# K rows of a long-convolution kernel: regrouped through DRAM in five reads a quarter, position zero joined to the skip weight, new issue order

## The chip, the cores and the metric

The program runs on one core of one Trainium2 chip. Times are device microseconds (us) of one execution. A kernel is run several times; the text gives the median and says how many runs there were. Most runs agree within 1 to 1.5%; a run more than 1.5% above the fastest of its kernel is marked slow and left out of ratios. Each kernel was also profiled once. A "span" is that execution from its first to its last instruction; it is about 2 us shorter than the time.

The engines: PE is TensorE (matmul), DVE is VectorE, ACT is ScalarE, POOL is GpSimd, SP is SyncE, which in this kernel does nothing but start DMA transfers. "SPq" in the profile is SyncE's sequencer at work on starting a transfer.

## The reference

Two independent halves are concatenated: a linear attention over x (2048 x 448, 16 heads), and a long convolution of u (2048 x 448) with a kernel K that a state-space model gives. Only the second half is touched:

```python
# _B_ref, cut
dt = jnp.exp(log_dt)[:, None];  A = A_re + 1j * A_im
l = jnp.arange(L)                                          # L = 2048
P = jnp.exp((dt * A)[:, :, None] * l[None, None, :])
K = jnp.einsum("dn,dnl,dn->dl", Cc, P, dt * Bc).real       # 448 channels x 2048 positions
... # FFT of K and u, both padded to 2L, product, inverse FFT
y = y + u * Dskip[None, None, :]
```

In bf16, `arange(2048)` holds only 641 different values, so the kernel computes K at 641 positions.

## The kernel before

The 448 channels are done in four quarters of 112. For each quarter, VectorE builds tables of powers, TensorE multiplies a "high" table (16 rows) with a "low" table (49 columns) to get K at position HI + LO, and ScalarE evicts that to the tile TS. In TS a partition is one high position of one of four channel groups. The spectrum matmuls want the K positions themselves on the partitions: the tile KT. `scatter_k` moves TS to KT. Position zero is the one that fits no block of 128 rows; it has a sixth block, KT[:, 5], with one row in use.

```python
N_LO = 49
K_ROWS = [(0, 0, 8, 0, 16), (1, 0, 8, 16, 32), (2, 8, 16, 16, 32), (3, 0, 16, 33, 41), (4, 0, 16, 41, 49)]
N_KT = 6
...
def dma(eng, o, i):
    e = {"S": nc.sync, "AD": nc.scalar, "G": nc.gpsimd}[eng]
    prog.add(eng, lambda: e.dma_start(out=o, in_=i))
...
def scatter_k(qt):                                  # one "set": 24 transfers, all on SyncE
    ts_, kt_ = TS[qt % 2], KT[qt % 2]
    for kt, h0, h1, l0, l1 in K_ROWS:
        for g in range(4):
            dma("S", kt_[:, kt, 28 * g:28 * g + 28], ts_[32 * g + h0:32 * g + h1, l0:l1, :])
    for g in range(4):                              # position zero: 4 transfers of 56 bytes
        dma("S", kt_[0:1, 5, 28 * g:28 * g + 28], ts_[32 * g:32 * g + 1, 32, :])
...
def query_side(sc):                                 # the attention half, cut
    ...
    dma("S", SCd[sc], SCT)                          # a small tile out to DRAM ...
    for h in range(4):                              # ... and back, spread over partitions
        dma("S", SB[28 * h:28 * h + 28], bass.AP(...SCd...))
    for s in range(2):
        mul(EQ[:, s], EQ[:, s], SB[:, 4 * s:4 * s + 4, :])     # VectorE waits for it
...
TERMS = ([(0, 0), (1, 1), (2, 2), (3, 3), (4, 5)], [(5, 3), (6, 4)])   # spectrum matmuls per K block
def load_f(m, at):                                  # the F tables of the spectrum, also SyncE
    t = sb(at, [128, 2, 7, 128])
    dma("S", t, F_d[m])
```

The program records its 1,198 operations and then issues them in a hand-tuned order (`ORDER`), with PSUM banks from a second list (`SLOTS`). SyncE works its transfers off in that order: one that waits, or that takes long to start, holds up all that come after it. In the profile of this kernel, SyncE was busy with the 24 starts of a set from 161.16 for 16.27 us, and started the query side's small transfer, next in its order, at 177.53, 0.10 us after the last of them.

The softmax here doesn't subtract the row's maximum and nothing guards it: scores larger than these inputs give would overflow.

Of the kernel before, what the change touches and what calls it, by code (L numbers as in the profile page):

```python
# [16 lines left out]
D_MODEL = 448  # L17
# [3 lines left out]
N_LO = 49  # L21
# [5 lines left out]
LO = [s * p for p in LO_ABS[:-1] for s in (1, -1)] + [16, 0, -16]  # L27
LO += [512 + p for p in LO[24:32]]
LO += [2 * LO[i] for i in (35, 37, 38, 40)]
LO += [512 + p for p in LO[41:45]]  # L30
assert len(LO) == N_LO
HI = [16 + 32 * a for a in range(N_HI)]
K_ROWS = [(0, 0, 8, 0, 16), (1, 0, 8, 16, 32), (2, 8, 16, 16, 32), (3, 0, 16, 33, 41), (4, 0, 16, 41, 49)]
N_KT = 6
# [6 lines left out]
def _row_positions():  # L41
    pos = np.full((N_KT, 128), -1)
    for kt, h0, h1, l0, l1 in K_ROWS:
        pos[kt] = [HI[h] + LO[lo] for h in range(h0, h1) for lo in range(l0, l1)]
    pos[5, 0] = HI[0] + LO[32]
    return pos

def _dft_tables():
# [10 lines left out]
    assert len(where) == 641 and set(where) == set(e.tolist())  # L59
    F = np.zeros((2, N_KT, 128, 4, 512))  # L60
    for blk in range(2):
        for l in range(1024):
            kt, r = where[int(e[1024 * blk + l])]
            even = np.exp(-1j * w * l) / 1024.0
            odd = np.exp(1j * (np.pi - w) * l) / 1024.0
            F[blk, kt, r] += np.stack([even.real, odd.real, even.imag, odd.imag])
    used = [(0, 0), (0, 1), (0, 2), (0, 3), (0, 5), (1, 3), (1, 4)]
# [4 lines left out]
    FT = FT.reshape(7, 128, 2, 8, 128).transpose(3, 1, 2, 0, 4)  # L72
# [31 lines left out]
def kernel(  # L104
# [22 lines left out]
    SUd = dram.tile([4, 128, 8, D_MODEL], BF16, name="SUd")  # L127
    SCd = dram.tile([4, 128, 128], BF16, name="SCd")
# [212 lines left out]
    for part, terms in enumerate(([("CreBre", DG), ("CimBim", DGN)], [("CreBim", DG), ("CimBre", DG)])):  # L341
        bs = prog.take("P", *((6, 7), (2, 3))[part])
        to_states(bs, [(prods[n], d) for n, d in terms])
        acopy(halves(CR[:, part, :]), two(bs))
    for n, k in enumerate(LOWP):
# [73 lines left out]
    dma("G", DSK, bass.AP(tensor=B_Dskip.tensor, offset=B_Dskip.offset, ap=[[0, 128], [1, D_MODEL]]))  # L419
# [3 lines left out]
    for kt in KT:  # L423
        mset(kt[:, 5, :], 0.0)
# [7 lines left out]
    def amps(qt):  # L432
        return sb((oW, 174336, 174336, oW)[qt], [128, 33, QC])
# [25 lines left out]
    def dampings(qt):  # L459
        A = amps(qt)  # L460
        for grp in range(2):
            p0, far_ = args(AT, qt, grp)
            for _, n, f, r0, step in GROUP[grp]:
                for sgn in (1, -1):
                    r = 2 * r0 + (sgn < 0) if r0 < 15 else (30, 32)[sgn < 0]
# [9 lines left out]
    def damp(qt, x0, w):  # L475
        A = amps(qt)
        smul(W[:, 1, 0:31:2, x0:x0 + w], A[:, 0:31:2, x0:x0 + w], -1.0)
        for part in (1, 0):
            for r, n, d, tr in ((0, 15, QC, 0), (30, 1, 2 * QC, 15)):
# [9 lines left out]
                else:  # L489
                    mul(view(o, [d, 2], [1, w]), view(a, [step, 2], [1, w]), view(b, [0, 2], [1, w]))  # L490
# [4 lines left out]
    def far(qt, x0, w):  # L495
# [10 lines left out]
        def four(part):  # L506
            return view(W[:, part, 35, x0:x0 + 1], [3 * QC, 2], [2 * QC, 2], [1, w])
# [7 lines left out]
        step(24, 33, 8)  # L515
# [3 lines left out]
        mul(view(W[:, 1, 41, x0:x0 + 1], [2 * QC, 2], [QC, 2], [1, w]), four(0), four(1))  # L519
        smul(rows_(1, 41, 4), rows_(1, 41, 4), 2.0)  # L520
        sub(rows_(0, 41, 4), sq[0], sq[1])
        step(41, 45, 4)
# [38 lines left out]
    def scatter_k(qt):  # L561
        ts_, kt_ = TS[qt % 2], KT[qt % 2]
        for kt, h0, h1, l0, l1 in K_ROWS:
            for g in range(4):
                dma("S", kt_[:, kt, 28 * g:28 * g + 28], ts_[32 * g + h0:32 * g + h1, l0:l1, :])
        for g in range(4):
            dma("S", kt_[0:1, 5, 28 * g:28 * g + 28], ts_[32 * g:32 * g + 1, 32, :])
# [100 lines left out]
    TERMS = ([(0, 0), (1, 1), (2, 2), (3, 3), (4, 5)], [(5, 3), (6, 4)])  # L668

    def load_f(m, at):  # L670
        t = sb(at, [128, 2, 7, 128])
# [153 lines left out]
    "0 2 15 4 3 5 22 21 12 14 9 6 11 10 28 17 27 7 8 13 1 19 29 16 20 30 18 31 32 33 23 43 24 36 44 25 51 26 159 "  # L825
    "52 91 157 89 37 92 90 56 53 34 99 55 97 127 66 100 129 35 54 75 57 85 98 58 81 76 88 61 82 79 80 87 77 45 78 "
    "84 83 86 40 209 38 227 64 46 65 59 236 70 218 41 68 60 62 69 130 103 63 161 104 160 93 212 101 95 102 162 42 "
    "165 96 221 49 94 128 208 354 39 50 226 105 210 47 106 107 48 357 72 112 108 211 109 113 73 158 74 71 213 114 "
    "214 110 215 217 136 111 230 117 115 135 219 116 220 180 119 164 181 67 222 122 223 118 224 183 120 182 235 "
    "184 121 123 124 185 186 239 187 216 125 225 245 229 126 188 228 244 237 231 254 238 232 133 233 253 134 240 "  # L830
    "234 248 139 241 247 242 246 257 249 243 140 137 250 256 251 255 189 252 138 258 131 262 163 132 141 259 271 "
    "260 265 191 264 261 177 274 273 147 178 276 267 298 263 148 268 277 190 266 166 179 272 172 142 269 170 193 "
    "174 171 270 192 143 275 144 168 278 173 279 145 280 176 146 152 169 167 175 283 205 207 153 282 281 206 285 "
    "194 284 286 154 195 287 200 197 290 432 433 288 293 435 434 301 436 289 300 292 303 299 291 302 294 316 201 "
    "155 307 295 296 199 326 156 304 203 305 202 297 368 306 310 343 318 438 309 437 319 312 308 198 317 321 311 "
    "320 325 322 196 323 473 313 204 314 149 474 370 329 372 369 475 315 150 476 327 151 479 328 477 470 478 330 "
    "324 471 531 481 331 332 472 334 371 480 333 337 335 336 525 338 346 344 345 429 347 348 527 418 339 431 340 "
    "341 349 342 424 350 427 374 351 423 425 422 353 426 356 352 420 355 484 483 421 373 358 485 482 359 419 534 "
    "376 428 375 378 362 379 377 486 380 363 488 487 489 430 490 366 381 528 383 367 360 491 364 361 492 382 365 "
    "493 677 526 384 511 385 494 439 392 495 530 390 532 397 391 529 394 440 520 499 496 498 395 497 521 441 533 "  # L840
    "398 443 407 536 399 535 389 518 387 516 403 442 513 386 396 519 408 515 388 445 406 393 402 514 444 415 404 "
    "512 537 500 540 412 517 539 416 501 400 414 401 411 413 538 405 541 542 410 409 543 504 570 417 630 631 459 "
    "451 460 450 454 453 452 447 458 449 544 446 448 456 462 545 457 522 461 455 505 463 546 465 469 464 467 468 "
    "466 547 506 524 633 632 634 523 548 508 507 569 502 509 671 678 549 679 566 550 668 672 567 674 669 673 616 "
    "553 551 554 676 552 627 670 675 718 625 568 681 682 572 680 683 715 626 624 620 684 635 622 686 685 629 555 "
    "712 503 556 628 709 510 619 687 898 559 688 689 618 899 690 636 571 623 557 617 560 558 574 563 621 573 576 "
    "561 577 575 578 564 579 691 562 761 581 719 565 580 582 720 583 716 750 692 710 637 693 602 711 604 717 608 "
    "600 714 639 603 713 695 694 697 696 598 638 754 722 724 641 721 601 751 723 610 762 593 613 725 763 727 605 "
    "726 728 590 729 757 730 585 760 596 731 758 640 756 732 614 759 592 752 611 584 755 733 595 699 734 753 612 "
    "597 698 606 594 607 589 599 643 737 736 588 738 735 609 642 586 615 587 702 767 591 659 660 661 664 665 658 "  # L850
    "666 662 663 657 656 654 646 667 655 648 706 645 653 703 647 652 644 649 650 651 700 707 764 740 704 701 739 "
    "814 705 925 765 708 741 815 745 817 766 743 853 816 860 768 769 924 742 747 744 818 770 748 842 854 846 746 "
    "956 749 855 771 856 820 861 772 773 864 775 774 825 881 776 866 777 865 862 778 863 821 871 779 823 843 888 "
    "872 873 780 819 847 781 845 844 828 829 848 791 849 790 831 824 830 926 928 850 927 827 832 793 867 851 795 "
    "834 852 833 822 882 835 826 883 889 884 836 892 891 837 857 893 894 839 806 874 859 807 858 890 802 895 838 "
    "788 897 896 868 785 870 841 869 875 840 878 876 786 880 929 800 879 877 808 885 787 886 930 803 887 931 798 "
    "792 932 809 933 804 943 810 783 811 782 942 801 799 784 805 796 789 944 794 1038 812 797 967 1070 1072 963 "
    "1073 1071 946 949 961 945 962 948 969 947 934 968 935 959 1057 953 965 957 960 970 950 1042 1004 964 813 "
    "1043 966 903 918 915 902 911 958 917 914 936 923 919 916 905 901 913 922 907 908 906 920 909 904 954 910 921 "
    "912 900 1041 971 951 955 939 937 1039 952 938 973 940 1040 941 972 974 976 975 1082 977 978 979 1078 981 980 "  # L860
    "982 1083 1005 1079 1084 1080 1085 1007 1076 1081 983 1074 984 985 987 986 1006 1002 1008 989 1009 1075 1077 "
    "1000 991 1010 1001 990 1011 992 998 1012 1013 999 1015 1014 988 1016 994 1017 1018 996 997 1019 993 1003 "
# [43 lines left out]
```

## Time and profile before

The median was 373.94 us (three runs, 373.57 to 377.03); the profiled run: span 373.4 us.

| engine | busy us | share of the span |
|---|---|---|
| DVE | 268.4 | 72% |
| PE | 252.3 | 68% |
| ACT | 209.7 | 56% |

No engine is full. DVE has the most work, and still stands idle for 373.4 - 268.4 = 105 us. The question is what it stands idle for. First the page of the kernel before: span, busy times, and the chain that ended last, by engine and by line.

```profile
span 373.4 us, 8746 instructions
PE 252.3 (68%) x3781; PEld 188.8 (51%) x3781; DVE 268.4 (72%) x324; ACT 209.7 (56%) x346; POOL 15.9 (4%) x32
PE 9%; SPq 8%; DVE 7%; issue 2%; DMA 1%; ACT 1%; DVEq 0%; ACTq 0%
PE psum L198 9%; SPq L213 8%; DVE sbuf L159 7%; DMA sbuf<-sbuf 1%; ACT sbuf L190 1%; DVEq L159 0%; ACTq L190 0%
```

Line 213 is the helper `dma`. The shares sum to 28% because the chain is followed back only to 267.4 us, so it covers the last two sets alone. That SyncE's sequencer has 8% of the last chain, with 1% for the transfers themselves, says that starting them is what counts. The view of line 213 gives one such start (count, then ns minimum/median/maximum, first and last start):

```profile
L213 SPq DMA_DIRECT2D sbuf<-sbuf x96: 567/602/987, 161.2 to 342.8; - x96
```

There are 96 of them (4 sets of 24), and each keeps SyncE for about 0.6 us. The packets of one such transfer took only 0.25 to 0.42 us in the trace, in the 68 of the 80 transfers of 128 packets whose packets stand apart there. The timeline of the kernel before shows the four places where that hurts (start us, length us, engine, what, count; in brackets the engine's idle time before it and what ended that):

```profile
161.16 16.27 SPq L213 DMA_DIRECT2D sbuf<-sbuf  x24
177.53 0.47 SPq L213 DMA_DIRECT2D SCd<-sbuf  x1
189.95 2.36 DVE L159 TENSOR_TENSOR sbuf<-sbuf 112x2048 bf16<-112x2048 bf16 x2 [11.93 <-DMA sbuf<-SCd]
...
241.54 2.45 SPq L213 DMA_DIRECT2D sbuf<-const  x4
246.06 5.84 PE L198 MATMUL psum<-sbuf 128*128 128x224 bf16 x44 [8.06 <-DMA sbuf<-const]
...
281.44 9.21 PE L198 MATMUL psum<-sbuf 128*128 128x112 bf16 x136 [0.84 <-DVE sbuf L159]
284.72 16.42 SPq L213 DMA_DIRECT2D sbuf<-sbuf  x24
302.56 9.82 PE L198 MATMUL psum<-sbuf 128*128 128x112 bf16 x259 [11.90 <-DMA sbuf<-sbuf]
...
326.66 16.70 SPq L213 DMA_DIRECT2D sbuf<-sbuf  x24
344.82 7.39 PE L198 MATMUL psum<-sbuf 128*128 128x112 bf16 x115 [12.11 <-DMA sbuf<-sbuf]
```

Set by set. The first set (161.2 to 177.4) has the query side's small transfer to DRAM behind it in SyncE's order; VectorE waits 11.93 us for what comes back. The second set (it ends at 240.2) has the loads of the F tables behind it (`sbuf<-const` at 241.54); PE waits 8.06 us. The third and the fourth are waited for directly: 11.90 and 12.11 us of PE. The view of waits adds them up for the whole span (us in total, times, longest):

```profile
PE psum L198 <- DMA sbuf<-sbuf: 24.0, 2, 12.1
PE psum L198 <- DMA sbuf<-const: 8.1, 1, 8.1
DVE sbuf L159 <- DMA sbuf<-SCd: 12.6, 2, 11.9
```

The sum of these three, 24.0 + 8.1 + 12.6 = 44.7 us, adds waits of two engines, so it is a count, and not by itself a proof of what they cost. It is called the *set waits* below: the time that PE or DVE stood waiting for K rows, or for something queued behind them.

### The profile page before, as it was taken

The numbers are of one execution on the slowest core, as the hardware profiler recorded it, in microseconds if no ns is written. First come the engines' busy times: TensorE is split into PE (matmuls) and PEld (weight loads), VectorE is DVE, ScalarE is ACT, GpSimd is POOL, SyncE is SP. The second block draws the span as 40 slices with busy tenths as digits, with TensorE's granted clock in tenths as the row PEclk, the third lists the DMA queues.
The fourth block names the chain that finished last, engine by engine and source line by source line (L and its number), as shares of the span: only waits on it lengthen the run. The fifth ranks groups of instructions, "written<-read, shape, count | busy, mean of one in ns | idle before, by whom it ended". The sixth has DMA issues, their size and how long they took to land. (4 is left out here: it accounts for less than half of the span.)

```text
span 373.4 us, 8746 instructions
## 1 busy us (share of the span) xinstructions
PE 252.3 (68%) x3781; PEld 188.8 (51%) x3781; DVE 268.4 (72%) x324; ACT 209.7 (56%) x346; POOL 15.9 (4%) x32
## 2 busy tenths in 40 slices
PE   2464999765988656788357569369949157960895
PEld 1343645533545425655125454158848156860894
DVE  3767798941799979169069769919997988593392
ACT  5697897777879865548509545068384112220421
POOL 8030100000000000000100000000000001000000
PEclk9998899999899558799559869969996759995899
DMA  8999052101011004001651523586153058321422
GB/s 193 216 286 140 2 164 79 51 0 49 13 38 51 0 3 101 4 10 10 162 215 54 100 59 56 140 281 182 50 199 116 8 107 302 106 34 27 83 52 50
DMA packets 50189, 35.40 MB, mean 95 GB/s; under 512 B 31880, under 2 KB 46232, under 8 KB 49768
## 3 DMA queue, kind: packets, MB, share of 16 engines
q1 hardware_dynamic: 47176, 27.58, 29.5%
q0 software_dynamic: 2976, 7.28, 6.5%
q8 instruction: 29, 0.48, 0.6%
q14 instruction: 8, 0.07, 0.1%
HBM read 26.77 MB, written 7.47 MB: 92 GB/s over the span
## 5 line engine op out<-in xcount | busy, mean ns | idle before, releaser
L198 PE MATMUL psum<-sbuf 128*16 128x49 bf16 (+9 forms) x3672 | 241.7, 267 | 102.1 <-DVE sbuf L159 25.8
L198 PEld LDWEIGHTS <-sbuf 128*16 128x16 bf16 (+4 forms) x3672 | 179.2, 112 | 164.6 <-issue 87.3
L159 DVE TENSOR_TENSOR sbuf<-sbuf 128x896 bf16<-128x896 bf16 (+11 forms) x235 | 221.4, 980 | 55.6 <-ACT sbuf L190 22.7
L190 ACT CAST sbuf<-psum 128x448 bf16<-128x448 f32 (+4 forms) x140 | 75.7, 568 | 119.8 <-PE psum L198 108.9
L187 ACT ACTIVATE sbuf<-psum 128x896 bf16<-128x896 f32 (+4 forms) x144 | 83.4, 655 | 28.9 <-PE psum L198 28.7
L177 DVE COPY sbuf<-psum 112x1024 bf16<-112x1024 bf16 (+2 forms) x16 | 7.4, 472 | 27.2 <-PE psum L198 10.0
L583 DVE TENSOR_REDUCE sbuf<-sbuf 128x32 f32<-128x896 bf16 x16 | 17.1, 1081 | 11.1 <-ACT sbuf L187 11.0
L187 ACT ACTIVATE sbuf<-psum,sbuf 128x896 bf16<-128x896 f32 (+3 forms) x28 | 21.6, 814 | 1.6 <-PE psum L198 1.5
L208 PE MATMUL psum<-sbuf 128*112 128x128 bf16 (+3 forms) x109 | 11.8, 279 | 15.2 <-DMA sbuf<-in_A_x_dram 5.7
L208 PEld LDWEIGHTS <-sbuf 128*112 128x112 bf16 (+3 forms) x109 | 10.1, 183 | 16.0 <-DMA sbuf<-in_A_x_dram 6.4
L187 ACT ACT_TABLE_LOAD x13 | 16.7, 1283 | 0.9 <-PEq L890 0.7
L187 ACT ACTIVATE sbuf<-sbuf 128x896 bf16<-128x896 bf16 (+3 forms) x13 | 11.4, 900 | 4.7 <-DVE sbuf L159 4.3
L184 DVE RECIPROCAL sbuf<-sbuf 128x32 bf16<-128x32 f32 (+1 forms) x20 | 7.7, 389 | 0.5
L213 POOL DMA_DIRECT2D sbuf<-SUd x4 | 2.1, 529 | 131.2 <-DVE sbuf L159 78.2
L190 ACT COPY sbuf<-psum 112x896 bf16<-112x896 bf16 x5 | 4.5, 909 | 4.7 <-PE psum L208 4.7
L213 POOL DMA_DIRECT2D sbuf<-in_B_u_dram x8 | 6.4, 808 | 14.0 <-PE psum L208 14.0
L171 DVE TENSOR_SCALAR sbuf<-sbuf 128x3584 bf16<-128x3584 bf16 (+4 forms) x11 | 6.7, 615 | 0.2
L213 POOL DMA_DIRECT2D sbuf<-const x3 | 1.7, 565 | 113.4 <-PE psum L198 113.4
L190 ACT CAST sbuf<-sbuf 128x1792 bf16<-128x1792 f32 x3 | 5.1, 1691 | 0.0
L159 DVE TENSOR_TENSOR sbuf<-psum,sbuf 128x128 f32<-128x128 f32 (+3 forms) x10 | 4.6, 489 | 0.0
L174 DVE SCALAR_TENSOR_TENSOR sbuf<-sbuf 128x64 f32<-128x64 f32 (+1 forms) x6 | 3.1, 510 | 0.1
L193 POOL MEMSET sbuf<- 128x16 bf16 (+3 forms) x7 | 1.6, 245 | 32.8 <-PE psum L198 19.9
(12 smaller groups left out, 8.8 us busy)
## 6 DMA issues: line engine op xcount, KB each, us to landing
sbuf<-const SPq DMA_DIRECT2D x16, 448.0 KB
SUd<-sbuf SPq DMA_DIRECT2D x8, 448.0 KB
sbuf<-SCd SPq DMA_DIRECT2D x16, 224.0 KB
sbuf<-SUd POOLq DMA_DIRECT2D x4, 896.0 KB, 5.2
sbuf<-const POOLq DMA_DIRECT2D x2, 1024.0 KB, 9.1
sbuf<-in_A_x_dram SPq DMA_DIRECT2D x4, 448.0 KB
out_dram<-sbuf SPq DMA_DIRECT2D x4, 448.0 KB
sbuf<-in_B_u_dram SPq DMA_DIRECT2D x16, 112.0 KB
```

The lines of the kernel that those rows point to most:

```text
L159: prog.add("V", lambda: nc.vector.tensor_tensor(out=o, in0=a, in1=b, op=op))
L171: prog.add("V", lambda: nc.vector.tensor_scalar_mul(o, a, s))
L174: prog.add("V", lambda: nc.vector.scalar_tensor_tensor(out=o, in0=a, scalar=s, in1=b, op0=op0, op1=op1))
L177: prog.add("V", lambda: nc.vector.tensor_copy(o, a))
L184: prog.add("V", lambda: low(lambda: nc.vector.reciprocal(o, a)))
L187: prog.add("A", lambda: nc.scalar.activation(o, a, fn, **kw))
L190: prog.add("A", lambda: nc.scalar.copy(o, a))
L193: prog.add("G", lambda: nc.gpsimd.memset(o, v))
L198: nc.tensor.matmul(o, lhsT=l, rhs=r, **kw)
L208: nc.tensor.transpose(o, i, idn)
L213: prog.add(eng, lambda: e.dma_start(out=o, in_=i))
L583: prog.add("V", lambda zk=zk, EK=EK: nc.vector.tensor_reduce(zk, EK.rearrange("p s (h f) -> p s h f", f=D_HEAD), axis=AX.X, op=ALU.add))
```

## The change

The intent: fewer starts. A quarter's K rows go out to a DRAM tile in two transfers and come back, position by position, in five. Position zero needs no row any more: K at position 0 is the sum over the states of Re(C B dt), and it multiplies u at the same time step, as the skip weight does. So it is summed once (a matmul with ones) and added to the skip weight. That takes the 49th table column, the sixth block, one of seven F terms, and the four single-row transfers away. The issue order and the bank list were made anew.

```diff
-N_LO = 49
+N_LO = 48
-K_ROWS = [(0, 0, 8, 0, 16), ..., (3, 0, 16, 33, 41), (4, 0, 16, 41, 49)]
-N_KT = 6
+K_ROWS = [(0, 0, 8, 0, 16), ..., (3, 0, 16, 32, 40), (4, 0, 16, 40, 48)]
+N_KT = 5
 ... (DFT tables, amplitudes and row numbers follow from it)
+    KTd = dram.tile([4, 3, 128, D_MODEL], BF16, name="KTd")
 ...
+    ones = sb(212544, [128, 128])
+    mset(ones, 1.0)
+    dma("G", DSK, bass.AP(tensor=B_Dskip.tensor, ...))          # moved up
+    bs = prog.take("P", 0)
+    mms([... (ones, view(CR[:, 0, ...])) ...])                  # sum of Re(C B dt) over the states
+    add(DSK, DSK, psum[:, bs[0], 0:D_MODEL])
 ...
     def scatter_k(qt):
         ts_, kt_ = TS[qt % 2], KT[qt % 2]
-        for kt, h0, h1, l0, l1 in K_ROWS:
-            for g in range(4):
-                dma("S", kt_[:, kt, 28 * g:28 * g + 28], ts_[32 * g + h0:32 * g + h1, l0:l1, :])
-        for g in range(4):
-            dma("S", kt_[0:1, 5, 28 * g:28 * g + 28], ts_[32 * g:32 * g + 1, 32, :])
+        kd = KTd[qt]
+        dma("S", kd[0:2].rearrange("b p x -> p b x"), ts_[:, 0:32, :].rearrange("p (b l) x -> p b (l x)", b=2))
+        k8 = kd[2].rearrange("p (b x) -> (p b) x", b=2)
+        dma("S", k8.rearrange("(b p) x -> p b x", b=2), ts_[:, 32:48, :].rearrange("p (b l) x -> p b (l x)", b=2))
+        for kt, h0, blk, n in ((0, 0, 0, 16), (1, 0, 1, 16), (2, 8, 1, 16), (3, 0, 2, 8), (4, 0, 3, 8)):
+            src = kd[blk, h0, 0:1] if n == 16 else k8[128 * (blk - 2), 0:1]
+            dma("S", kt_[:, kt, :].rearrange("p (g x) -> p g x", g=4),
+                bass.AP(tensor=src.tensor, offset=src.offset, ap=[[28, 128], [32 * 28 * n, 4], [1, 28]]))
 ...
-    TERMS = ([(0, 0), (1, 1), (2, 2), (3, 3), (4, 5)], [(5, 3), (6, 4)])
+    TERMS = ([(0, 0), (1, 1), (2, 2), (3, 3)], [(4, 3), (5, 4)])
 ... (ORDER and SLOTS: all new)
```

## The prediction

> **What bounds the kernel now.** No engine is full: the page's part 1 has DVE busy 268.4 us of a 373.4 us span, PE 252.3, ACT 209.7. DVE carries most, yet idles for 105 us. The chain of waits shows the last third: SPq L213 is 7.8% of the span, in two runs of 24 SyncE issues of about 0.6 us (284.8 to 300.5 and 327.3 to 342.7 us). Those are the transfers that lay K rows on partitions, 24 a quarter. The timeline shows PE idle 290.7 to 302.6 (11.9 us) and 332.7 to 344.8 (12.1 us) behind them, DVE idle 339.2 to 351.6 (12.4 us) behind the second. The first set (161.2 to 177.4) holds up the query side's small DRAM transfer on the same queue: DVE idles 178.0 to 190.0. The second (223.6 to 240.2) delays the F tables: PE idles 238.0 to 246.1, DVE 242.2 to 250.9. About 40 us of DVE idling hang on the four sets, 7 of it knock-on of the third.
>
> **What changes, costed.**
> - A set is now two writes to DRAM and five reads. Before: 24 issues x 0.65 us + 1.98 us landing, 17.6 us. After, an estimate: two issues, 1.2; DRAM round trip 1.6 to 3.4 (the query side's write to its first read's issue in this trace[...]); five reads at 0.4 to 0.6 an issue; 2 landing. The 2,560 packets of 56 bytes stay: 128 took 0.25 to 0.40 us, so a read of 512 may take 1.0 to 1.6 us and queue behind the one before[...]. A set: 7.5 to 12 us, about 9. Gain 8 us a set, and SyncE is freed of some 45 us of issuing.
> - Position zero leaves the tables: 49 to 48 columns in 1,792 matmuls (part 5: 45 us; about 0.8 us), one of seven F terms fewer (about 3.6 us of PE), F loads 448 to 384 KB each. DVE stays near 267.
> - New order: the last quarter's set is again last; spectrum, convolution and store after it take what they took, 28.6 us from 344.8 to the end. DVE may now be the limit there: two convolutions are 29 us of DVE work, plus 7 of PE, ACT and store.
>
> **On the critical path.** Of the 40 us, halved sets return about 18; better hiding on a free queue and the smaller spectrum 5 to 10 more, minus what DVE and PE take over. I expect 24 us less: 350 us, range 336 to 363. Faster by over 2% 0.9, within 2% 0.07, slower 0.03.
>
> **What would show it.** Right: SPq's share of the final chain falls to under 3%; a set spans under 12 us from first write to last landing; the two PE gaps near 12 us shrink to under 6; DVE busy stays 265 to 268, its idle time falls by over 15 us; SyncE issues fall from 195 to 127. Wrong: reads take over 1.6 us each where PE waits, or one sticks behind an unrelated store or load on SyncE's in-order queue.
>
> **What would make me wrong.** A slow receipt of the write; reads issued behind loads that wait for the convolution's buffers (the new order has two such); the new start-up order; a gap that ACT (busy 73% between 60 and 160 us) opens instead.

The sum came to 24 us: 18 us back of the 40, 5 to 10 more, less an unnamed part that DVE and PE take over. The costs in it are estimates from the profile before. The 3.6 us of the F term fit the 16 of 256 matmuls of 128x224 (31.1 us busy) and 32 of 832 of 128x112 (48.7 us) that go with it: 1.9 + 1.9 = 3.8 us.

## The result

The changed kernel is correct. Its median was 334.46 us (four runs, 332.25 to 336.75), against 375.49 us (four runs) before. Ratios here and below are the mean time of one kernel's fast runs over that of the other's of the same rounds, so not quite the ratio of the medians: 0.892, 95% interval 0.883 to 0.902. So 41 us were gained where 24 had been predicted, and 334.46 us lies just below the predicted range of 336 to 363. The page after:

```profile
span 333.4 us, 8578 instructions
PE 249.7 (75%) x3741; PEld 186.4 (56%) x3741; DVE 267.5 (80%) x325; ACT 205.6 (62%) x340; POOL 15.6 (5%) x31
PE 37%; DVE 28%; DMA 15%; ACT 13%; issue 4%; SPq 2%; DVEq 0%; ACTq 0%
```

DVE does the same work, 267.5 us, and its idle time fell from 105.0 to 333.4 - 267.5 = 65.9 us. That fall, 39.1 us, is nearly the whole gain. The view of waits after has this left of the three lines above; no line says that PE waits for K rows:

```profile
PE psum L198 <- DMA sbuf<-const: 0.6, 1, 0.6
DVE sbuf L159 <- DMA sbuf<-SCd: 2.4, 1, 2.4
```

The set waits fell from 44.7 to 3.0 us, within 1 us of the gain. The view of the tile KTd after gives the new transfers (count, ns minimum/median/maximum of a start), and under it who waited for them (nobody in this profile) and the time from start to landing, which the trace has for six of the 28:

```profile
L213 SPq DMA_DIRECT2D sbuf<-KTd x20: 367/505/1209, 159.1 to 298.7; - x20
L213 SPq DMA_DIRECT2D KTd<-sbuf x8: 370/425/1203, 153.8 to 292.4; - x8
who waited for it (us, times):
DMA to landing us min/median/max: 2.0/2.8/5.4
```

And the timeline after, in the first and in the last quarter:

```profile
153.85 0.89 SPq L213 DMA_DIRECT2D KTd<-sbuf  x2
159.07 1.54 SPq L213 DMA_DIRECT2D sbuf<-KTd  x3
163.53 0.95 SPq L213 DMA_DIRECT2D sbuf<-KTd  x2
...
291.96 0.88 SPq L213 DMA_DIRECT2D KTd<-sbuf  x2
296.21 2.97 SPq L213 DMA_DIRECT2D sbuf<-KTd  x5
296.28 28.50 DVE L159 TENSOR_TENSOR sbuf<-sbuf 128x3584 bf16<-128x3584 bf16 x32 [0.96 <-ACT sbuf L190]
300.83 9.78 PE L198 MATMUL psum<-sbuf 128*128 128x112 bf16 x192 [0.16 <-DVE sbuf L159]
```

The last set now keeps SyncE for 0.88 + 2.97 = 3.85 us instead of 16.70. DVE works from 296.3 to 324.8 without a gap while it goes on, and PE has no gap longer than half a microsecond from 295 to 310. The last 8.6 us of the span come after DVE has finished.

### The profile page after: what moved, and what is told of

It reads as the page before. It is cut to its first block, busy times and chain, and to the rows that moved or that the text cites. A ratio compares the mean times of both kernels' runs of the same rounds, so it can differ in the third digit from the quotient of the medians.

```text
span 333.4 us, 8578 instructions
## 1 busy us (share of the span) xinstructions
PE 249.7 (75%) x3741; PEld 186.4 (56%) x3741; DVE 267.5 (80%) x325; ACT 205.6 (62%) x340; POOL 15.6 (5%) x31
## 3 DMA queue, kind: packets, MB, share of 16 engines
q0 software_dynamic: 2976, 7.28, 7.1%
## 4 chain that ended last, share of the span: by engine, by line
PE 37%; DVE 28%; DMA 15%; ACT 13%; issue 4%; SPq 2%; DVEq 0%; ACTq 0%
PE psum L198 36%; DVE sbuf L159 22%; ACT sbuf L187 7%; DMA sbuf<-in_A_x_dram 5%; DMA sbuf<-in_B_C_re_dram 4%; ACT sbuf L190 4%; DMA sbuf<-SCd 4%; DVE sbuf L592 4%; SPq L213 2%; DVE sbuf L184 1%; DMA sbuf<-const 1%; ACT L187 1%; DMA SCd<-sbuf 1%; PE psum L208 0%; DVE sbuf L177 0%
## 5 line engine op out<-in xcount | busy, mean ns | idle before, releaser
L198 PE MATMUL psum<-sbuf 128*16 128x48 bf16 (+10 forms) x3632 | 237.7, 265 | 63.3 <-ACT sbuf L187 21.5
L159 DVE TENSOR_TENSOR sbuf<-sbuf 128x896 bf16<-128x896 bf16 (+13 forms) x235 | 219.5, 975 | 32.9 <-ACT sbuf L187 16.3
L198 PEld LDWEIGHTS <-sbuf 128*16 128x16 bf16 (+4 forms) x3632 | 175.3, 112 | 125.9 <-issue 70.4
L187 ACT ACTIVATE sbuf<-psum 128x448 bf16<-128x448 f32 (+4 forms) x140 | 83.9, 659 | 33.0 <-PE psum L198 31.7
L208 PE MATMUL psum<-sbuf 128*112 128x128 bf16 (+3 forms) x109 | 13.0, 305 | 16.4 <-DMA sbuf<-in_A_x_dram 7.3
L208 PEld LDWEIGHTS <-sbuf 128*112 128x112 bf16 (+3 forms) x109 | 11.6, 207 | 17.0 <-DMA sbuf<-in_A_x_dram 8.0
L159 DVE TENSOR_TENSOR sbuf<-sbuf,psum 112x448 bf16<-112x448 bf16 (+1 forms) x2 | 1.2, 621 | 4.3 <-issue 3.4
```

The lines of the kernel that those rows point to most:

```text
L159: prog.add("V", lambda: nc.vector.tensor_tensor(out=o, in0=a, in1=b, op=op))
L187: prog.add("A", lambda: nc.scalar.activation(o, a, fn, **kw))
L198: nc.tensor.matmul(o, lhsT=l, rhs=r, **kw)
L208: nc.tensor.transpose(o, i, idn)
```

## The experiments

Three things were changed at once, and the predicted gain had been 17 us too small. The questions were which part gives what, and why more came back than the halving of a set had been thought to give.

The theory: SyncE's time to start a set is all that matters, and a stall is what a set takes *beyond* a slack that PE and DVE have anyway; when the set gets shorter than the slack, the whole stall goes. Rivals: (a) the new issue order does a good part of it; (b) what helps is the way through DRAM, or the fewer and other packets, and not the fewer starts; (c) a stall is in proportion to the set, and something else gave the rest.

All kernels below keep to the reference's outputs, but for old_regroup_no_tiny, which leaves a term out. "Old order" means the order and bank list of the kernel before, with the transfers of a set replaced where they stood; "new order" that of the changed kernel. Runs in the same block were on the same chip, with the kernel before beside them: 375.57 us (7 runs) for the first four, 376.11 us (7 runs) for the next four, 374.31 us (11 runs) for the last four (the lines of the table are in this order).

| run | order | position zero | a set | median us | ratio to before (95%) | set waits us |
|---|---|---|---|---|---|---|
| (before) | old | in the tables | 20 + 4 small | 375.57 | 1 | 44.7 |
| after_again | new | joined | 2 + 5 through DRAM | 334.63 | 0.891 (0.883 to 0.899) | 1.9 |
| old_order_all | old | joined | 2 + 5 through DRAM | 332.85 | 0.883 (0.876 to 0.891) | 1.6 |
| new_order_small | new | joined | 20 small | 354.09 | 0.943 (0.937 to 0.949) | 18.2 |
| old_order_regroup | old | in the tables | 2 + 5 through DRAM + 4 small | 346.79 | 0.923 (0.915 to 0.931) | 13.3 |
| old_order_pos0 | old | joined | 20 small | 351.91 | 0.941 (0.933 to 0.950) | 27.8 |
| old_regroup_no_tiny | old | left out | 2 + 5 through DRAM | 336.64 | 0.896 (0.889 to 0.903) | 3.7 |
| old_pos0_two_queues | old | joined | 20 small, half by GpSimd | 331.96 | 0.883 (0.876 to 0.890) | 3.7 (second take) |
| new_reads_twice | new | joined | 2 + 10 through DRAM | 361.47 | 0.964 (0.957 to 0.971) | 24.4 |
| old_regroup_two_queues | old | joined | 2 + 5 through DRAM, split | 331.85 | 0.887 (0.884 to 0.890) | 2.0 |
| old_pos0_two_queues_b | old | joined | 20 small, half by GpSimd | 332.36 | 0.888 (0.885 to 0.892) | 3.7 |
| new_delay_4 | new | joined | 2 + 5, 4 dummies | 335.49 | 0.894 (0.889 to 0.898) | 5.6 |
| new_delay_12 | new | joined | 2 + 5, 12 dummies | 356.45 | none, see below | 18.1 |

The set waits are, for every kernel, the sum of PE's waits for `sbuf<-sbuf`, `sbuf<-KTd` and (on the line of the tables and spectra) `sbuf<-const`, and DVE's for `sbuf<-SCd`. Time less set waits lies between 324 and 338 us in all rows: most of what differs between these kernels is set waits, though not all: these differences still spread over 14 us.

### after_again: the changed kernel once more

No edit.

> The changed kernel once more, as the yardstick of this chip. Both theories: 332 to 337 us, ratio 0.89 to the kernel before.

Measured: 334.63 us (four runs, 333.21 to 336.99). The result holds in a second block, beside other runs of the kernel before. In this second profile the set waits are 1.9 us instead of 3.0, and PE once waited for K rows, 0.5 us.

### old_order_all: everything but the new order

The changed code with the old `ORDER` and `SLOTS`: the two writes and five reads stand where the first seven of the 24 small transfers stood, and the few new operations next to what they need. No line of code differs from the changed kernel.

> All of the change except its order: five reads and two writes a set, position zero in the skip weight, 48 columns, but the instructions stand in the old order (the seven transfers take the places of the first seven of the old twenty-four). Theory S (the short sets alone did it): the four stalls vanish here too, 334 to 345 us. Theory O (the new order hides what the short sets leave, as the prediction did not count on): only about half of the 40 us of stalls comes back, as predicted, 350 to 358 us, with PE gaps of 4 to 6 us left behind the third and fourth set.

Measured: 332.85 us (four runs, one slow), ratio 0.883, as fast as the changed kernel within the intervals, and 1 us below the range of theory S. The new order is worth nothing beyond what the other two parts give; rival (a) falls. The timeline shows why the first stall is gone here:

```profile
159.90 0.90 SPq L213 DMA_DIRECT2D KTd<-sbuf  x2
161.99 2.56 SPq L213 DMA_DIRECT2D sbuf<-KTd  x5
169.49 0.34 SPq L213 DMA_DIRECT2D SCd<-sbuf  x1
```

The set has SyncE until 164.55. The query side's transfer (`SCd<-sbuf`) starts at 169.49, 5 us later, because what it stores was not ready sooner. Before, it started at 177.53, one tenth of a microsecond after the set's last start. A set could take 169.5 - 159.9 = 9.6 us here before it delayed anything. And the timeline of VectorE shows what bounds the end: from 254.7 to 320.9 it has no gap longer than about 0.1 us, the last stretch of that being this line.

```profile
281.02 39.93 DVE L159 TENSOR_TENSOR sbuf<-sbuf 128x448 bf16<-128x448 bf16 x48
```

### new_order_small: the new order without the way through DRAM

```diff
     def scatter_k(qt):
-        (two writes to KTd, five reads)
+        for kt, h0, h1, l0, l1 in K_ROWS:
+            for g in range(4):
+                dma("S", kt_[:, kt, 28 * g:28 * g + 28], ts_[32 * g + h0:32 * g + h1, l0:l1, :])
```

The four small transfers of each block stand where its read stood.

> The new order and position zero, but the twenty small transfers of a set are back, four where each read stood, no DRAM. Theory S: the long sets stall the engines again, 355 us or more. Theory O: the new order hides most of them, 336 to 348 us.

Measured: 354.09 us, 1 us short of what theory S had asked for. The twenty starts cost 19.5 us over the changed kernel, in the new order as in the old (old_order_pos0 is 19.1 us over old_order_all, in another block). All three kinds of set wait are back in the view of waits:

```profile
DVE sbuf L159 <- DMA sbuf<-SCd: 8.8, 2, 6.6
PE psum L198 <- DMA sbuf<-sbuf: 7.1, 3, 4.9
PE psum L198 <- DMA sbuf<-const: 2.3, 3, 1.1
```

### old_order_regroup: the way through DRAM alone

The kernel before, with its 49 columns, its F tables and its order; only the twenty transfers of `scatter_k` are replaced, and the four for position zero stay:

```diff
     def scatter_k(qt):
-        for kt, h0, h1, l0, l1 in K_ROWS:
-            for g in range(4):
-                dma("S", kt_[:, kt, 28 * g:28 * g + 28], ts_[32 * g + h0:32 * g + h1, l0:l1, :])
+        (the two writes, with columns 33:49, and the five reads of the change)
         for g in range(4):
             dma("S", kt_[0:1, 5, 28 * g:28 * g + 28], ts_[32 * g:32 * g + 1, 32, :])
```

> The kernel before with one part of the change alone: two writes and five reads a set (and the four tiny transfers of position zero, still there), old order, 49 columns. Theory S: nearly as fast as the whole change, 340 to 350 us, since position zero is worth little. Theory O: 352 to 362 us.

Measured: 346.79 us, so 28.8 us of gain by this part alone. The set waits fell by 44.7 - 13.3 = 31.4 us. The view of the helper's line shows what a start costs in each kind of transfer:

```profile
L214 SPq DMA_DIRECT2D sbuf<-KTd x20: 359/494/511, 164.8 to 311.4; - x20
L214 SPq DMA_DIRECT2D sbuf<-sbuf x16: 722/753/1451, 167.4 to 314.4; - x16
```

A read of 512 packets of 56 bytes takes SyncE 0.49 us to start. One of the transfers for position zero, which moves 56 bytes, takes 0.75 us: more than anything else in the set, for 1/512 of the data.

### old_order_pos0: position zero alone

The changed code with the old order and twenty small transfers, as in new_order_small, where the 24 stood.

> Old order and small SBUF-to-SBUF transfers, with position zero joined to the skip weight as the only change: twenty transfers a set instead of twenty-four, 48 columns, six F terms. Theory L (length: what a set gets shorter comes back at each of the four places where an engine waits for it): the four tiny issues were 0.8 us each, 3.3 us a set, so 13 us, and about 3 of PE work: 356 to 363 us. Theory T (the smaller tables are all that position zero is worth, as the prediction had it): 369 to 373 us.

Measured: 351.91 us, so 24.2 us of gain by this part alone (from 376.11), more than both theories had asked for, and far more than the smaller tables are worth (next run). The set waits fell by only 44.7 - 27.8 = 16.9 us, so some 7 us of this gain are not set waits; the smaller tables may be about half of them, the rest was not traced. Here too the sets are still what PE and DVE wait for, only less:

```profile
PE psum L198 <- DMA sbuf<-sbuf: 16.1, 2, 9.1
PE psum L198 <- DMA sbuf<-const: 5.9, 1, 5.9
DVE sbuf L159 <- DMA sbuf<-SCd: 5.8, 3, 4.6
```

Against the kernel before of their own blocks, the parts alone give 28.8 and 24.2 us, 53.0 together; both at once give 42.7. They do not add, as is to be expected where each shortens the same sets: once a set is inside its slack, a shorter one gives nothing more.

### old_regroup_no_tiny: the way through DRAM, and no transfer for position zero

This one is old_order_regroup without the four single-row transfers, so K at position zero is missing from the result. (The term is small enough that the comparison with the reference still passed; that is not a proof of correctness, the term is left out.) It has the 49 columns and seven F terms of the kernel before.

```diff
-        for g in range(4):
-            dma("S", kt_[0:1, 5, 28 * g:28 * g + 28], ts_[32 * g:32 * g + 1, 32, :])
```

> The regrouped kernel of old order with 49 columns and seven F terms, but without the four tiny transfers of position zero: its row stays zero, so the result lacks that term and is wrong on purpose. Theory L: most of the 14 us between that kernel (346.8) and the whole change in old order (332.9) were the tiny transfers: 333 to 339 us. Theory T: they were the smaller tables, 343 to 347 us.

Measured: 336.64 us. From old_order_regroup (346.79) to old_order_all (332.85) are 13.9 us; this run splits them. The sixteen transfers, 0.75 us each to start, are 346.79 - 336.64 = 10.2 us of it (16 x 0.75 = 12.0 us of SyncE). The smaller tables and spectra are the other 336.64 - 332.85 = 3.8 us. (This run lies in another block than the other two; the kernel before differs by 0.5 us between the blocks, and the intervals of the last two ratios overlap, so the 3.8 us are not clear of noise.) This run is also the cleanest measure of shorter sets alone, as order, tables and spectra are those of the kernel before: 376.11 - 336.64 = 39.5 us.

### old_pos0_two_queues and old_pos0_two_queues_b: no DRAM, half the starts on another engine

This is the test between the theory and rival (b). The transfers stay small and stay in SBUF; every second one is started by GpSimd, which is idle at that time (in the profile before, POOL was busy for 0.53 us in the second set and not at all in the other three).

```diff
# against old_order_pos0
-                dma("S", kt_[:, kt, 28 * g:28 * g + 28], ts_[32 * g + h0:32 * g + h1, l0:l1, :])
+                dma("SG"[g % 2], kt_[:, kt, 28 * g:28 * g + 28], ts_[32 * g + h0:32 * g + h1, l0:l1, :])
```

> As old_order_pos0, no DRAM, but every second small transfer is issued by GpSimd, whose queue is idle then. Theory I (what costs is one sequencer issuing at 0.65 us each): a set takes some 8 to 9 us instead of 14, so 335 to 347 us. Rival D (the 56-byte packets or the landing of SBUF-to-SBUF transfers cost, and DRAM regrouping cures that): within 4 us of old_order_pos0.

Measured: 331.96 us (four runs; the profiled one was slow), 3 us below the range of theory I. It was taken again.

> The same kernel as old_pos0_two_queues, taken again because its profile had fallen in the slow state and because it was the fastest so far (331.96 us): no DRAM, twenty small transfers a quarter split over SyncE and GpSimd, old order, position zero joined. If it holds: 330 to 334 us, ratio 0.875 to 0.890 to the kernel before, and a set of 8 to 10 us from first issue to last packet with no PE gap over 4 us behind it. If it was luck: over 336 us.

Measured: 332.36 us (six runs, one slow), ratio 0.888, as fast as the changed kernel. The view of the helper's line in the second take:

```profile
L213 SPq DMA_DIRECT2D sbuf<-sbuf x40: 560/604/1208, 157.9 to 297.3; - x40
L213 POOL DMA_DIRECT2D sbuf<-sbuf x40: 536/615/1371, 158.2 to 294.0; - x40
```

A start takes as long as before, 0.60 us on SyncE and 0.62 on GpSimd, but ten in a row instead of twenty. That took 351.91 to about 332 us, with the same twenty transfers a set and no DRAM, so the way through DRAM is not needed. The packets of GpSimd's half did change: its queue (q0 of the page) carried 4,256 packets and 7.58 MB instead of the 2,976 and 7.28 of the kernel before, 1,280 packets more for its forty transfers of 7 KB, 32 each on average, where one of SyncE's took 128 of 56 bytes in the trace of the kernel before. But packets are not what the change saves: the traces of the kernel before and of the changed kernel both have 10,240 packets of 56 bytes, and before, those of one transfer that stand apart were done in 0.25 to 0.42 us, well within the 0.64 us from one start to the next. Rival (b) falls: what counted was the number of starts in a row on one sequencer.

### new_reads_twice: a longer set, first attempt

Meant to lengthen each set by five starts of 0.5 us: every read from DRAM is started twice.

```diff
-            dma("S", kt_[:, kt, :]..., bass.AP(...))
+            for _ in range(2):
+                dma("S", kt_[:, kt, :]..., bass.AP(...))
```

> The changed kernel with each of the five reads of a set issued twice (the same bytes again), so that a set is some 3 us longer on its queue. Theory L with slack: the fourth set has 3 us to spare, the second under 1, so 334 to 339 us. If every microsecond on that queue still counted four times: 344 us or more.

Measured: 361.47 us, far more than expected, by a fault of the experiment. Both copies write the same bytes, so the second waits on SyncE until the first has landed, as the view of waits shows:

```profile
SPq L213 <- DMA sbuf<-KTd: 47.7, 20, 5.5
```

So a set grew by 47.7 / 4 = 12 us of waiting, on top of the five starts. It says that long sets stall again (set waits 24.4 us) and nothing about the slack.

### new_delay_4 and new_delay_12: a longer set, cleaner

The changed kernel; after each of the first four reads of a set, one or three transfers of 56 bytes from DRAM to unused DRAM, which nothing waits for.

```diff
+    XXd = dram.tile([4, 12, D_MODEL], BF16, name="XXd")                  # 4 in new_delay_4
 ...
+            for d in range(3 if kt < 4 else 0):                          # 1 in new_delay_4
+                dma("S", XXd[qt, 3 * kt + d:3 * kt + d + 1, 0:28], x2[0:1, 0:28])
```

> The changed kernel with one dummy transfer of 56 bytes from DRAM to DRAM, which nothing waits for, after each of the first four reads of a set: a cleaner form of the flawed run with doubled reads. It makes a set longer by four issues, 0.5 to 0.8 us each, so 2 to 3.2 us. Theory (a set has some slack before the work that needs it: about 0.8 us in the second quarter, 7.5 in the third, 3.6 in the fourth, none that counts in the first): 1 to 4 us longer than the changed kernel, 335.5 to 338.5 us. Rival (what a set takes is paid in full in each of the four quarters): 8 to 13 us longer, 342 to 347 us.

> As new_delay_4 with three dummy transfers after each of the first four reads: a set becomes 6 to 9.6 us longer. Theory (stall is set length less slack): the second quarter pays 5 to 9 us, the third 0 to 2, the fourth 2.5 to 6: 8 to 17 us longer than the changed kernel, 342 to 352 us, and per added us more than in new_delay_4. Rival (paid in full everywhere): 24 to 38 us longer, 358 to 372 us, in proportion to new_delay_4.

A dummy keeps SyncE for 0.75 us in both (the view of the helper's line in new_delay_12):

```profile
L214 SPq DMA_DIRECT2D XXd<-in_A_x_dram x48: 726/747/1552, 160.1 to 324.2; - x48
```

So a set was longer by 4 x 0.75 = 3.0 us in one kernel and by 12 x 0.75 = 9.0 us in the other. Three us more cost nothing that can be told in the time: 335.49 us (six runs, two slow), ratio 0.894, inside the interval of the changed kernel; the rival "paid in full" had asked for 342 to 347. Nine us more cost 15 to 22: 349.85 us in the fastest of four runs, 356.45 in the median. The other three runs lie over 1.5% above the fastest and are marked slow, so there is no ratio, and the size stays rough; the median is above the 342 to 352 that the theory had asked for, and below the 358 to 372 of the rival. The profile (of one of the slower runs) has the three waits back, 18.1 us of them:

```profile
DVE sbuf L160 <- DMA sbuf<-SCd: 9.1, 2, 7.1
PE psum L199 <- DMA sbuf<-KTd: 7.1, 2, 4.1
PE psum L199 <- DMA sbuf<-const: 1.9, 3, 1.2
```

By quarter the expectation was wrong. It had counted nothing for the first and 5 to 9 us for the second. The timeline has the largest single wait in the first:

```profile
176.41 4.30 DVE L160 TENSOR_TENSOR sbuf<-sbuf 112x2048 bf16<-112x2048 bf16 x3 [7.12 <-DMA sbuf<-SCd]
```

In the new order the loads that VectorE waits for there stand between the reads, behind six of the twelve dummies; in the profile of new_delay_4, behind two of four, it waited 1.9 us. The second quarter has 0.7 us of waits, the third 1.2. In the fourth PE waited 0.7 us with 3 us more and 4.1 + 3.0 = 7.1 us with 9 us more: a slack of about 2 us both times. (Both profiles are of runs marked slow, so these waits are rough.)

Twelve us added over the four sets cost about nothing, 36 cost 15 to 22. A cost in proportion to the set, rival (c), does not do that; a slack does. The closer test of (c) is under "Why the prediction was wrong".

### old_regroup_two_queues: a try for a faster kernel

old_order_all, with one of the two writes and two of the five reads started by GpSimd.

```diff
-        dma("S", k8.rearrange("(b p) x -> p b x", b=2), ...)
+        dma("G", k8.rearrange("(b p) x -> p b x", b=2), ...)
-            dma("S", kt_[:, kt, :].rearrange("p (g x) -> p g x", g=4),
+            dma("SG"[kt % 2], kt_[:, kt, :].rearrange("p (g x) -> p g x", g=4),
```

> A try for a version that beats both: the regrouping through DRAM and the joined position zero in the old issue order (332.9 us), with one of the two writes and two of the five reads of each set issued by GpSimd instead of SyncE. Theory (the sets no longer stall anything that counts; what is left is VectorE work and other waits): a set loses 1 to 2 us, and the time stays at 330 to 334 us, within 1% of 332.9. Rival (what is left of the sets still stalls PE about one for one): 4 sets shorter by 1 to 2 us give 326 to 329 us.

Measured: 331.85 us (six runs, all fast, 329.76 to 332.91), the lowest median of all, but its ratio of 0.887 (0.884 to 0.890) overlaps that of every other kernel without set waits. It lies 0.8% below the changed kernel's two medians, in another block: not shown to be faster. With 1.6 us of set waits in old_order_all there was nothing left to gain by shorter sets, as the theory says. What bounds these kernels now lies elsewhere: 267.5 us of DVE work in a span of 328.7, with DVE busy for 90% or more of every fortieth of the span from 205 to 320.

## Why the prediction was wrong

**Where the time would come from: right.** The prediction put about 40 us of DVE's idling down to the four sets, by way of SyncE's starts. DVE's idle time fell by 39.1 us, the set waits by 41.7, the time by 41.0. That they agree this closely is partly luck: in old_order_pos0 the waits fell by 16.9 us and the time by 24.2. Most of the named signs came: SPq's share of the last chain is 2% (predicted: under 3), both 12 us gaps of PE before K rows are gone, DVE's work is 267.5 us, starts on SyncE fell from 195 to 127.

**What a set costs: about right, on the cautious side.** In old_order_all the first set took 0.90 for two starts, 1.19 until the first read, 2.56 for five reads: 4.65 us, and a landing (2.0 us at the least, 2.6 in the median of the five reads whose landing the changed kernel's trace has), against the predicted 7.5 to 12. The feared 1.0 to 1.6 us for a read of 512 small packets mostly did not come: the reads were started every 0.5 us, and in the changed kernel's trace, taken 512 by 512 in order of time, the packets took 0.4 to 0.9 us for fourteen of the twenty reads, 1.0 to 1.5 for four, and 2.0 and 3.1 for the other two. One sign was wrong: "a set spans under 12 us" does not hold in the changed kernel, whose new order puts other transfers between the writes and the reads (in the first quarter from 153.85 to the landing of the last read at about 169.3, 15.5 us). No wait for K rows came of it in that profile.

**The step that failed: "Of the 40 us, halved sets return about 18".** By its words it takes a stall as a share of its set. Shorter sets alone returned 39.5 us (old_regroup_no_tiny), more than twice that. The runs show a stall as the set's length less a slack. The numbers were in the profile before. In the last quarter SyncE began the set at 326.66, and PE idled only from 332.71 to 344.82: the first 6 us of the set were hidden behind PE's own work, and the stall was the 12 us beyond. In the third quarter the same: PE worked until 290.66, 5.9 us into the set, and stalled for 11.90. A set of the predicted 9 us leaves 3 us of each of these, not half of 12, and next to nothing of the first quarter's stall, where a set may take about 9 us (9.6 in old_order_all; in the kernel before, the small transfer's data was ready at 170.0, 8.9 us after the set's start). In the second quarter, set less wait is 6.6 to 8.5 us in the three old-order kernels that wait there for over 1 us (before: 16.6 - 8.1), so 9 us would leave 0.5 to 2.4. With hindsight this estimate leaves 6.5 to 8.4 us of the 44.7, a gain of 36 to 38 us. The prediction had even written "Gain 8 us a set", 32 us for four, and then counted 18.

The third quarter tests this against a share of the set, in the five old-order kernels whose sets SyncE starts alone. A set is counted from its first start to the end of its last one:

| run | set us | PE's wait us | set less wait | wait / set |
|---|---|---|---|---|
| before | 16.4 | 11.9 | 4.5 | 0.72 |
| old_order_pos0 | 13.0 | 9.1 | 3.9 | 0.70 |
| old_order_regroup | 8.4 | 3.4 | 5.0 | 0.41 |
| old_order_all | 5.8 | 0.6 | 5.3 | 0.10 |
| old_regroup_no_tiny | 5.3 | 1.5 | 3.8 | 0.28 |

The difference stays within 3.8 to 5.3 us, while the ratio falls from 0.72 to 0.10: rival (c) falls. In all five PE had 5.4 to 6.6 us of other work from the start of the set: that is the slack. The shortest set, in the timeline:

```profile
262.62 0.97 SPq L214 DMA_DIRECT2D KTd<-sbuf  x2
265.07 2.82 SPq L214 DMA_DIRECT2D sbuf<-KTd  x5
270.07 2.08 PE L199 MATMUL psum<-sbuf 128*128 128x112 bf16 x39 [1.46 <-DMA sbuf<-KTd]
```

new_delay_4 and new_delay_12 show it from the other side: 3 us more in every set for nothing that can be told in the time, 9 us more for 15 to 22.

**"Better hiding on a free queue and the smaller spectrum 5 to 10 more": half right by number.** Smaller tables and spectra gave 3.8 us, not clear of noise (estimated in the parts: 0.8 + 3.6). The new order gave nothing (332.85 us without it, 334.5 with it).

**"Minus what DVE and PE take over": did not come.** The prediction took something off for a new limit. DVE did become the limit at the end (no gap from 296.3 to 324.8 in the changed kernel, none over about 0.1 us from 254.7 to 320.9 in old_order_all), but only once the stalls had gone: DVE was still idle for 65.9 us afterwards, and the time fell by as much as the set waits did, so nothing that it took back can be seen.

**Position zero was worth more than its tables.** The prediction costed it as table columns and an F term. On top of the regrouping it brought 13.9 us, of which 10.2 were four starts per set of 0.75 us each, for 56 bytes apiece. (The prediction has these starts in its sum, among the 24 of a set.)

**What stays open.** The first quarter fits less closely: the small transfer started 7.5 us late, and VectorE waited 11.9 us; from that start to VectorE's took 12.4 us, against 8.7 in old_order_all, and why was not looked into. The clock granted to PE was 0.861 in the profile before and 0.887 and 0.892 in the two after, and PE was busy for 252.3 us before and 249.7 and 244.6 after; what part of that the clock has was not separated from the smaller tables. The size of the loss in new_delay_12 is known only as 15 to 22 us. That a start of a single-row transfer takes longer than one of 512 packets (0.75 against 0.49 us) is measured, and its cause isn't.

## What to carry to other kernels

When a sequencer's track is solid with small transfers, count starts, not bytes. Here a set took SyncE the number of starts in a row times the time of one (24 starts of 0.60 us and the gaps between them 16.4 us, twenty 13.0 us, the seven of the last set of the changed kernel 3.85 us), and it fell on everything behind it, even on transfers that had nothing to do with it (11.93 us of VectorE for the query side's tile, 8.06 us of PE for the F tables). Before predicting, add up the lines of waits that end in those transfers *and in the ones queued behind them*, and read from the timeline how much of a set passes before anyone waits. What was shortened came off the stall about one for one (in the third quarter set less wait stayed at 3.8 to 5.3 us for sets of 5.3 to 16.4 us), until the slack was reached; then nothing more was to be had (splitting the starts of old_order_all too took 331.85 us against its 332.85, which is not shown to be faster). Try the cheap remedy too: giving half of the starts to an idle engine's queue, with position zero joined, did as much here (332.36 us) as the whole regrouping through DRAM (334.46 us).

## What the traces measured of starts and packets

- A start against its packets: 0.60 us a start against 0.25 to 0.42 us of packets (where they stand apart), in runs of twenty and 24. Splitting the starts over two engines took the kernel from 351.91 to about 332 us.
- How long a start kept SyncE, by shape: 0.60 us (median) for 128 packets of 56 bytes from 8 or 16 partitions, 0.49 us for 512 packets of 56 bytes from DRAM to 128 partitions, 0.75 us for a single row of 56 bytes (in the trace 28 packets of 4 bytes, 14 of which would carry the row). Of these three the single row was the slowest, and the most data the fastest; why, no run here shows.
- Small pieces from DRAM: reads of 512 pieces of 56 bytes were started every 0.5 us, the five of twenty whose landing the trace has landed 2.0 to 5.4 us after their start (median 2.6), and no engine waited for them in the first profile of the changed kernel (one wait of 0.5 us in the second). A throughput was not measured.
